# The first two-level projection loads its fourth weight part into batch 1's turned x, ahead of its first product

## The chip, the cores and the metric

The kernel runs on one core of one Trainium2 chip. The metric is device time in microseconds (us) for one execution of the whole kernel. In what follows TensorE does the matrix products, VectorE and ScalarE the elementwise work and the copies out of the product banks, and SyncE and ScalarE each issue DMAs on a queue of their own. GpSimd has little to do here.

## The reference

An attention without softmax is followed by a feed-forward net of products. All of it is in 32-bit floats; the weights come in as 64-bit floats and are converted in the kernel.

```
# q, k, v: (8 batches, 8 heads, 576 tokens, 64)
kv  = einsum('bhsd,bhse->bhde', k, v)
out = einsum('bhsd,bhde->bhse', q, kv)
x   = out / sqrt(mean(out*out, axis=-1) + 1e-6) * g_norm     # -> x: (4608 tokens, 512)
a   = x @ w1                                                 # w1, w2: (512, 1024)
b   = x @ w2
h   = a * b @ w3                                             # w3: (1024, 1024)
result = h @ w_out                                           # w_out: (1024, 512)
```

## The kernel before

**The algebra.** The kernel folds w3 and w_out into one 1024 x 512 matrix (`w3o_sb`) at the start, so per token only two steps are left: the gates (x times w1 and w2, and the product of the two) and the projection (times the folded matrix). Both use Strassen's scheme in Winograd's form: seven block products in place of eight, with sums of blocks made on VectorE. From batch 2 on parts of the gates, and from batch 1 on the whole projection, apply the scheme on two levels: each of the seven outer products is itself made of seven inner ones.

**The groups.** The tokens are worked off in nine groups of 512: the first 512 tokens of each of the eight batches, and one group made of the 64 last tokens of every batch. The loop over `groups` runs the gates of group T, then its projection, and in the gaps of both (`between`, and slots hung on single copies) the attention of the next batch: k·v, q·kv, the norm, and the turning of x and q into the layout in which TensorE wants them. The turning goes through DMA transposes: `turn_by_dma` splits the words into planes by a copy (L321 or L323), SyncE issues the transpose (L325), and a copy puts the words together again (L335).

**The first two-level projection.** Group 0 (batch 0) is projected on one level. While that runs, `prepare_b` makes from the folded matrix the seven right-hand sides of the outer products, each with the sums that its inner products need, and stores them to HBM (`w3o_l2`), seven parts of 128 x 1792 words, 896 KB. Every later projection reads these parts back, one for each outer product, in order. The first projection to do so is batch 1's (T = 1), `project_twice` with `done[T] = 0`. Counting the products from 1, product i reads part i.

**The homes of the parts.** `streams` holds three homes of part size: two in the old place of `w3o_sb` (streams 0 and 1) and one in a `raw` tile (stream 2). A home is free for the next part when the product that read it is done. From the second projection on there is a fourth home: the turned x of the batch whose gates have just ended (`xT[...]`), which takes the fourth part at the start of the projection. Batch 1's xT is read by the matmuls of the gates (L778), for the last time in the product of a12 and b21, the last but one of the stage. Its buffer goes to batch 3's x later.

**Who issues a part.** `load_b` issues the next part each time it is called (L1248). In the first projection parts 4 and 6 go out on ScalarE's queue and the others on SyncE's; the first three are issued well ahead, within the gates of T = 1.

**The order.** SyncE, TensorE and GpSimd run their instructions in the order in which the kernel writes them. VectorE does so too in the last part of the gates and in the projection. ScalarE's instructions are put in order by a scheduler, when the kernel is built. Each engine takes its own in that order, so what stands behind a waiting instruction waits too. DMAs share eight completion semaphores in turn; a DMA also waits for the one that held its semaphore before.

**Around the projection.** The lines that the steps touch are these. `copy_seven` (L1121, L1122) copies the two product banks of an outer product to `slots`; a product that writes these banks again waits for it. `gates` ends with c21: ScalarE copies one half (L946), VectorE multiplies (L948). VectorE then makes the left-hand sums of the inner products (L1284 to L1287, and L858, L859), and, between them, the sums of the next batch's x (L848). After a product VectorE adds its banks to the sums kept before (L1125, L1126). After the fourth product SyncE issues loads of q for the batch after next (L95), and after the fifth to the seventh it loads weight parts of the next group's gates (L1018).

The kernel's order of one projection, without what is the same:

```
        if done[T]:
            load_b()
        r1 = products(0)
        ...
        products(3, r2)
        if not done[T]:
            load_b()
```

Of the kernel before, what the change touches and what calls it, by code (L numbers as in the profile page):

```python
# [22 lines left out]
def kernel(  # L23
# [711 lines left out]
    def w3_by_dma(c):  # L735
        natural, to = chunks[:, c, 0, :], place_w3(1, c).rearrange("p m f -> p (m f)")
        return turn_by_dma(
            [natural], to, natural, [to], nc.scalar.copy, split=nc.vector.tensor_copy
        )
# [131 lines left out]
    o_sbs, ab_sums, w3o_sums, streams, inner_sums, in_a_row = [], [], [], [], [], []  # L871
# [172 lines left out]
    def gates_of_two(T, between=lambda: None):  # L1044
# [36 lines left out]
        def load(w, n):  # L1081
            last = max(at for (v, m, _), at in BLOCKS.items() if (v, m) <= (w, n))
            if last + 1 >= (len(loaded_w) - len(streams) + 1) * IN_PART:
                load_w()
            if (w, n) == (1, len(PRODUCTS) - 1):
                for _ in range(3):
                    load_b()
# [146 lines left out]
    def load_b():  # L1234
        n = len(loaded_b)
        if n == ALL_B:
            return
        i = n % 7
        t = streams[n % 3] if n < 7 else streams[(i + 1 if i < 3 else i) % 3]
        if n >= 7 and i == 3:  # L1240
            done_with = xT[groups[1 + n // 7]]
            t = done_with.rearrange("p i j r n -> p (i j r n)")[:, 0:PART]

        part = {ALL_B - 2: 6, ALL_B - 1: 7}.get(n, n % 7)

        queue = nc.scalar if i in ((3, 5) if n < 7 else (4, 6)) else nc.sync
        if n + 1 < ALL_B:
            queue.dma_start(out=t, in_=w3o_l2[part])  # L1248
        else:
            t = t[:, 0:1024]  # L1250
            queue.dma_start(out=t, in_=w3o_l2[part, :, 0:1024])
        loaded_b.append(t)
# [43 lines left out]
    def project_twice(T, last, ahead, load_after):  # L1296
# [12 lines left out]
        def products(n, ps=None):  # L1309

            new = ps is None or n == 5 or last and n == 6
            if ps is None:
                ps = [bank(ps_mm, "mm").rearrange("p (i n) -> p i n", n=P) for _ in range(2)]
            a11, a12, a22, s1, s2, s4, s3 = inner[n]
            w = loaded_b[7 * done[T] + (5 if last and n == 6 else n)]
            b = w[:, 0:1024].rearrange("p (f n) -> p f n", n=N)
            b11, t3, b21, b22 = (
                b[:, 2 * i:2 * i + 2, j * P:(j + 1) * P] for i in range(2) for j in range(2)
            )
            t1, t2, t4 = (  # L1320
                w[:, 1024 + 256 * i:1280 + 256 * i].rearrange("p (c n) -> p c n", n=P)
                for i in range(3)
            )
            seen = set()
            for place, x, y in (
                (0, a11, b11), (3, a12, b21), (1, a22, t4), (2, s1, t1), (6, s2, t2), (5, s4, b22),
                (4, s3, t3),
            ):
                for c in range(2):
                    nc.tensor.matmul(  # L1330
                        ps[place // 4][:, place % 4, :], lhsT=x[:, c, :], rhs=y[:, c, :],
                        start=new and place // 4 not in seen,
                        stop=(c == 1),
                        skip_group_check=True,
                    )
                    seen.add(place // 4)
            return ps
# [41 lines left out]
                store_block(0, 0, m, m + 1, queue, cols)  # L1379


        if done[T]:
            load_b()
        r1 = products(0)
        p1 = keep("p1", r1)
        load_b()
        r2 = products(1)
        p5 = keep("p5", r2)
# [6 lines left out]
        for f in ahead:  # L1395
            f()
        products(3, r2)
        if not done[T]:
            load_b()
        for f, *args in slots.pop(("proj", "loads"), []):  # L1400
            f(*args)
        if last:
# [29 lines left out]
    done = {}  # L1432
# [14 lines left out]
    with tc.manual_schedule(  # L1447
# [63 lines left out]
        for c in range(KF):  # L1511
# [9 lines left out]
            if c < KF - 2:  # L1521
# [12 lines left out]
                if c in SPLIT:  # L1534
                    t = turns[SPLIT[c]] = w3_by_dma(SPLIT[c])
# [49 lines left out]
    for n, T in enumerate(groups):  # L1585
# [119 lines left out]
        if T:  # L1705
            project_twice(
                T, last, [] if last else combine_x(groups[n + 1]),
                load_w if not last and groups[n + 1] in IN_TWO else load_b,
            )
            in_order.__exit__(None, None, None)  # L1710
            continue
# [46 lines left out]
```

## Time and profile before

| | |
|---|---|
| median of 3 runs | 739.49 us (738.42 to 739.94) |
| profiled execution | 738.91 us, of which the span is 736.8 us |
| TensorE busy in the span | 731.3 us, 99% |
| VectorE, ScalarE, GpSimd busy | 85%, 52%, 3% |
| granted TensorE clock | 1.000 |
| DMA | 170.44 MB, mean 231 GB/s |
| weight parts from `w3o_l2` (L1248), 896 KB each | 40 on SyncE, 15 on ScalarE; 4.4 to 8.7 us from issue to landing |

The profile is one execution, taken by the hardware profiler. Rows of the timeline give the start in us from the start of the span, the length, the engine, the line and the tiles (written <- read); "SPq" and "ACTq" are DMA issues on SyncE's and ScalarE's queue, where the length is that of the issue and not of the transfer. In brackets stands how long the engine was idle before, and what ended that. The ends of matmuls are modelled.

### The profile page before, as it was taken

Reading aid. Unit: us, or ns where it says so; the run is one execution under the profiler, and the core shown is the slowest. Engines: PE = TensorE matmul, PEld = TensorE weight load, DVE = VectorE, ACT = ScalarE, POOL = GpSimd, SP = SyncE. Lnnn points to the kernel's source line nnn. Section 1 sums busy time; section 2 is a strip of 40 time slices with the busy share of each in tenths; the row PEclk is TensorE's granted clock in tenths of the full one; section 3 lists DMA queues with packets and bytes.
Section 4 is the critical chain, followed back from the end, with each engine's and each line's share of the span. In section 5 each row is a group of like instructions: output and inputs, shape, how many; then the busy total and the mean of one; then the engine's idle time right before and its main releaser. Section 6 shows DMA issues by size and latency. Waiting matters only on the chain.

```text
span 736.8 us, 16930 instructions
## 1 busy us (share of the span) xinstructions
PE 731.3 (99%) x6873; PEld 658.4 (89%) x6873; DVE 627.5 (85%) x1259; ACT 381.1 (52%) x660; POOL 23.1 (3%) x30
## 2 busy tenths in 40 slices
PE   8999999999999999999999999999999999999998
PEld 6455788888899999999999999999999999999998
DVE  7988898868879689969996899689879987997797
ACT  7888778315652676167517761675177313212321
POOL 0000000220001000000010001000001000000000
PEclk9999999999999999999999999999999999999999
DMA  8999925599999598869987988698748862565454
GB/s 309 355 338 249 285 94 154 157 329 274 326 299 321 172 286 245 277 159 276 259 275 166 302 237 278 157 299 242 253 115 217 221 209 87 187 214 158 135 196 142
DMA packets 138769, 170.44 MB, mean 231 GB/s; under 512 B 81220, under 2 KB 114116, under 8 KB 138692
## 3 DMA queue, kind: packets, MB, share of 16 engines
q1 hardware_dynamic: 136240, 155.02, 71.4%
q10 hardware_dynamic: 2452, 14.35, 5.8%
q8 instruction: 54, 0.88, 0.5%
q14 instruction: 23, 0.19, 0.1%
HBM read 130.55 MB, written 20.71 MB: 205 GB/s over the span
## 4 chain that ended last, share of the span: by engine, by line
PE 98%; DMA 1%; DVE 0%; SPq 0%; issue 0%; ACT 0%; DVEq 0%
PE mm L778 37%; PE mm L1330 23%; PE mm L1072 21%; PE mm L747 8%; PE at L778 3%; PE at L362 3%; PE mm L440 1%; PE at L440 1%; PE at L731 1%; DMA raw<-in_moe_w_out_dram 1%; PE at L1373 0%; PE at L459 0%; PE at L382 0%; PE mm L302 0%; SPq L219 0%; PE at L476 0%
## 5 line engine op out<-in xcount | busy, mean ns | idle before, releaser
L1121 ACT COPY slots<-mm 128x512 f32<-128x512 f32 x88 | 51.6, 586 | 127.3 <-PE mm L1330 83.1
L778 PE MATMUL mm<-xT,w_sb 128*128 128x256 f32 x432 | 99.3, 379 | 0.0
L778 PEld LDWEIGHTS mm<-xT,w_sb 128*128 128x128 f32 x432 | 81.4, 190 | 11.1 <-issue 0.5
L778 PE MATMUL mm<-xc,ws 128*128 128x256 f32 x328 | 74.4, 379 | 0.0
L778 PEld LDWEIGHTS mm<-xc,ws 128*128 128x128 f32 x328 | 62.3, 190 | 8.5
L796 ACT COPY slots<-mm 128x512 f32<-128x512 f32 x58 | 34.0, 585 | 69.5 <-PE mm L778 64.7
L747 PE MATMUL mm<-chunks,ab 128*128 128x512 f32 (+1 forms) x136 | 59.2, 573 | 0.3 <-DVE chunks L193 0.3
L1125 DVE TENSOR_TENSOR slots<-mm,slots 128x512 f32<-128x512 f32 x66 | 45.2, 685 | 16.3 <-PE mm L1072 15.9
L1122 ACT COPY slots<-mm 128x384 f32<-128x384 f32 x88 | 42.3, 481 | 25.0 <-PE mm L1330 22.1
L1072 PE MATMUL mm<-ws,w3o_sb 128*128 128x128 f32 x350 | 54.0, 275 | 0.0
L1330 PE MATMUL mm<-w3o_sb,ab 128*128 128x128 f32 x368 | 48.8, 276 | 0.0
L408 DVE TENSOR_REDUCE inv<-sq 128x8 f32<-128x512 f32 (+1 forms) x40 | 24.6, 629 | 26.9 <-ACT sq L407 26.9
L1072 PEld LDWEIGHTS mm<-ws,w3o_sb 128*128 128x128 f32 x350 | 46.4, 192 | 0.0
L1330 PEld LDWEIGHTS mm<-w3o_sb,ab 128*128 128x128 f32 x368 | 45.4, 192 | 0.5
L1330 PE MATMUL mm<-w3o_sb,raw 128*128 128x128 f32 x340 | 43.5, 275 | 0.0
L747 PEld LDWEIGHTS mm<-chunks,ab 128*128 128x128 f32 x136 | 24.0, 190 | 21.0 <-issue 17.9
L1330 PEld LDWEIGHTS mm<-w3o_sb,raw 128*128 128x128 f32 x340 | 40.7, 192 | 0.0
L778 PE MATMUL mm<-xT,ws 128*128 128x256 f32 x160 | 38.1, 381 | 0.0
L1126 DVE TENSOR_TENSOR slots<-mm,slots 128x384 f32<-128x384 f32 x66 | 36.3, 551 | 2.0 <-PE mm L1330 1.9
L778 PE MATMUL mm<-xc,w_sb 128*128 128x256 f32 x152 | 36.6, 384 | 0.0
L778 PEld LDWEIGHTS mm<-xT,ws 128*128 128x128 f32 x160 | 30.1, 190 | 4.3 <-ACT slots L796 0.2
L335 ACT COPY xT<-xn 128x1024 uint16<-128x1024 uint16 x26 | 30.2, 1167 | 3.5 <-DMA xn<-xT 3.5
(247 smaller groups left out, 1664.3 us busy)
## 6 DMA issues: line engine op xcount, KB each, us to landing
w3o_sb<-w_l SPq DMA_DIRECT2D x21, 896.0 KB, 6.2
w3o_sb<-w3o_l SPq DMA_DIRECT2D x18, 896.0 KB, 6.6
raw<-in_moe_w_dram SPq DMA_DIRECT2D x31, 512.0 KB, 7.8
raw<-w3o_l SPq DMA_DIRECT2D x15, 896.0 KB, 4.9
w3o_sb<-w3o_l ACTq DMA_DIRECT2D x14, 896.0 KB, 4.8
k_sb<-in_k_dram SPq DMA_DIRECT2D x16, 576.0 KB, 4.9
v_sb<-in_v_dram SPq DMA_DIRECT2D x16, 576.0 KB, 5.8
q_sb<-in_q_dram SPq DMA_DIRECT2D x32, 256.0 KB, 5.4
```

The source lines that it names most:

```text
L335: copy(words(dst), src)
L362: nc.tensor.matmul(ps[r * D:(r + 1) * D, :], lhsT=k_sb[rows, r, cols], rhs=v_sb[rows, r, cols], start=(j == 0), stop=(j == JS - 1),)
L408: adds["norm"] = nc.vector.tensor_reduce(out=inv[:, i], in_=sq.rearrange("p (h d) -> p h d", d=D), axis=AX.X, op=ALU.add)
L747: nc.tensor.matmul(sums_ps[half][m][:, cols], lhsT=w3T[half, c][:, m, :], rhs=chunks[:, c, 1, cols], start=(c == 0 and cols.start == 0), s ...
L778: nc.tensor.matmul(ps[:, u, :], lhsT=lhsT(a_name, u, c), rhs=rhs(b_name, c),  start=(u == 0 and c == 0 and new), stop=(c == chunks - 1), s ...
L796: copies.setdefault(name, []).append(nc.scalar.copy(t, ps))
L1072: nc.tensor.matmul(ps[place // 4][:, place % 4, :], lhsT=x, rhs=y, start=new and place // 4 not in seen, stop=True, skip_group_check=True,)
L1121: nc.scalar.copy(z[:, 0:4], ps[0])
L1122: return nc.scalar.copy(z[:, 4:7], ps[1][:, 0:3])
L1125: nc.vector.tensor_add(z[:, 0:4], ps[0], z[:, 0:4])
L1126: nc.vector.tensor_add(z[:, 4:7], ps[1][:, 0:3], z[:, 4:7])
L1330: nc.tensor.matmul(ps[place // 4][:, place % 4, :], lhsT=x[:, c, :], rhs=y[:, c, :], start=new and place // 4 not in seen, stop=(c == 1), ...
```

## The change

In the first two-level projection the fourth part is loaded into the home of batch 1's turned x, and the load is issued ahead of the first product in place of after it. The first three parts change homes (streams 1, 2, 0 in place of 0, 1, 2), so that each later part finds its home free one product sooner: part 5 after product 1, part 6 after product 2, part 7 after product 3. The call after the fourth product goes. Queues (ScalarE for parts 4 and 6) and the order of the parts stay. The later projections are as before.

```diff
     def load_b():
         n = len(loaded_b)
         if n == ALL_B:
             return
         i = n % 7
-        t = streams[n % 3] if n < 7 else streams[(i + 1 if i < 3 else i) % 3]
-        if n >= 7 and i == 3:
+        t = streams[(i + 1 if i < 3 else i) % 3]
+        if i == 3:
             done_with = xT[groups[1 + n // 7]]
             t = done_with.rearrange("p i j r n -> p (i j r n)")[:, 0:PART]
...
-        if done[T]:
-            load_b()
+        load_b()
         r1 = products(0)
         p1 = keep("p1", r1)
         load_b()
...
         products(3, r2)
-        if not done[T]:
-            load_b()
         for f, *args in slots.pop(("proj", "loads"), []):
             f(*args)
```

In the built program this moves two instructions on ScalarE and none on SyncE. Part 4's issue stands on ScalarE ahead of the L946 copy of c21, where it stood behind the second L335 copy of x; part 6's issue stands ahead of the copies after product 3, where it stood behind the two L335 copies of q that follow them. On SyncE parts 5 and 7 keep their places and wait for one product less.

## The prediction

> **What bounds the kernel now.** I read the page first, for the bound. Its chain of waits says TensorE:
>
> ```profile
> PE 98%; DMA 1%; DVE 0%; SPq 0%; issue 0%; ACT 0%; DVEq 0%
> ```
>
> Then the same chain in order of time, cut to the edited stage. Columns: start, length, what:
>
> ```profile
> 204.83 6.04 PE mm L778 x28
> 210.87 21.89 PE mm L1330 x196
> 232.75 3.46 PE mm L778 x16
> ```
>
> Nothing stands between these pieces. The first projection (196 matmul records, seven products of 28) runs from 210.87 to 232.75 in 21.89 us; the undisturbed ones at 283.49 and 643.64 take 21.93 and 21.88. So no part of the weights comes late in this execution, and an earlier load has no TensorE idle time to remove. The price, if any, must come from queues that the moved loads share. So I read ScalarE and SyncE in this window (start, length, engine, line, tiles; "q" is the issue of a DMA):
>
> ```profile
> 210.95 0.37 ACT L946 COPY c<-mm 128x256 f32<-128x256 f32 x1 [4.42 <-PE mm L778]
> 213.54 1.16 ACT L335 COPY xT<-xn 128x1024 uint16<-128x1024 uint16 x1 [2.22 <-DMA xn<-xT]
> 214.09 0.36 ACTq L1248 DMA_DIRECT2D w3o_sb<-w3o_l  x1
> 214.60 0.58 ACT L1121 COPY slots<-mm 128x512 f32<-128x512 f32 x1
> ```
>
> ```profile
> 198.30 5.36 SPq L325 DMA_TRANSPOSE xn_left<-qT_left  x1
> ...
> 207.01 4.31 SPq L325 DMA_TRANSPOSE xn<-xT  x2
> 211.42 2.61 SPq L325 DMA_TRANSPOSE q_sb<-qT  x2
> 217.15 6.58 SPq L1248 DMA_DIRECT2D w3o_sb<-w3o_l  x2
> ```
>
> ScalarE's 213.54 row is the one to see: it waits 2.22 us for two transposing DMAs, and behind it in its order stand the copies (L1121, L1122) that empty product 1's banks. Last, VectorE, which has little air:
>
> ```profile
> 212.30 0.41 DVE L948 TENSOR_TENSOR ab<-c,mm 128x256 f32<-128x256 f32 x1
> 212.63 0.68 DVE L1284 TENSOR_TENSOR inner_sums<-raw 128x512 f32<-128x512 f32 x1
> ...
> 214.68 0.68 DVE L1287 TENSOR_TENSOR raw<-raw 128x512 f32<-128x512 f32 x1
> ```
>
> **What the old timing leaves.** I count products from 1; each lasts 3.13 us, and by TensorE's rows they start at 210.71, 213.83, 216.96, 220.08, 223.21, 226.34 and 229.46. Issue plus landing (DMA issues of that stretch): part 4, 214.09 + 5.0 = 219.1; part 5, 217.15 + 4.6 = 221.8; part 6, 220.45 + 4.9 = 225.4; part 7, issued at 217.15 + 6.58 - 0.34 = 223.39, + 5.4 = 228.8. The margins are 1.0, 1.4, 0.9 and 0.7 us: thin, all positive.
>
> **The edits.** *First three parts.* The same three loads of 896 KB stand at the same place of SyncE's order (196.16 to 197.86), in other homes. Cost 0.
>
> *Part 4's load.* It moves to ScalarE's order ahead of the L946 copy. The changed program's order gives its waits: the last product that reads batch 1's xT (the last but one of that stage, ended by 210.87 - 1.73 = 209.14), and the landing of the xn_left transpose, with which it shares a completion semaphore. That one is issued at 198.30 and takes 12.0 us (DMA issues), so 210.3. The issue then goes at 210.3 instead of 214.09. No row shows ScalarE issuing a DMA while SyncE is inside a transpose. Near bound: the 0.36 of row 214.09, done at 210.7, before the L946 copy can start (210.95): 0. Far bound: it stands until SyncE's transposes are issued (211.42 + 2.61 = 214.03), and the copy is 3.1 us late. Who waits for that: VectorE's product at L948 has 212.30 - (210.95 + 0.37) = 0.98 us to spare, and the four sums behind it end at 214.68 + 0.68 = 215.36 for a block that TensorE starts at 216.51, 1.15 more. So 2.1 of the 3.1 us are free and 1.0 would stop product 2. I take 0, since the nearest row is an issue of this very size on this very queue.
>
> *Its data.* The old load's 896 KB came after the transposes: the DMA rate is 279 GB/s at 212 to 213, falls to 112 at 215 to 216, and is 421 at 216.5 to 218. Issue to data is about 1.0 us, so the data now starts near 211.4, on top of the second xn transpose and the two of q. Those move 128x1024 two-byte words each, 262 KB, about 1.0 us at 257 to 287 GB/s. Bounds for their delay: 0, if the load gets only what the transposes leave; above, if it goes wholly first, 3.0 us, its time from data start to 218.1 in the old place; at its full rate of 421 GB/s, 917 KB / 421 = 2.2. The L335 copy would start that much after 213.54. From there to the end of the first bank's copy (214.60 + 0.58 = 215.18) nothing can shrink, and product 3, which writes that bank again, starts at 216.96. So 1.78 us of delay are free, and the rest stops TensorE one for one: 0 to 1.2 us. I take 2.1, just under the full-rate value: 2.1 - 1.78 = 0.3 us. Next in line are the subtractions that read xT (VectorE, 219.39, L848; the second L335 copy ends at 216.63: 2.8 spare) and q's copies (220.66, behind a product-3 copy): both hidden.
>
> The Trainium skill speaks against mixing these two. "DMA: Bandwidth & Descriptors", section "Queues, rings and completion order", says that each DMA engine goes round-robin, packet by packet, over the queues with work; so a load from ScalarE's queue would take its turn beside SyncE's transposes and not wait behind them. Read as equal shares, the 1.65 us of transposes left at 211.4 would take 3.3, a delay of 1.65 and no stall: the sum would be 0.0 instead of 0.3. No row of this trace has both queues full at once.
>
> *Part 6's issue* (ScalarE) now stands ahead of product 3's first copy, L1121 at 219.00, before which ScalarE idles 1.36 us; 0.36 fits in. Without that cover it would cost 0.36. *Parts 5 and 7* (SyncE) pass no other instruction, they only wait for a product one earlier. Behind part 7 stand the two q loads (223.84), which may go about 1 us sooner. *The home:* batch 3's x is written there only in the next stage, after 232.75; part 4 is read out at 223.2. All three cost 0.
>
> **Sum.** The profiled execution took 738.91 us, 736.82 of span (736.8 on the page) and 2.09 around it. 738.91 + 0.3 = 739.2. The median of the runs shown is 0.58 above it: 739.49 + 0.3 = **739.8**. A measurement of this kernel tells about 0.2% from no change, 1.48 us, so the borders are 738.0 and 741.0.
>
> **The rivals.** *Transposes stand behind the load (slower).* One mechanism: the xn transposes are held on the DMA queues. Up to 1.78 us it is free; it decides from 1.78 + 1.48 = 3.3 us. The bound above gives 3.0 if only the data is held. If the issue of the second transpose is stretched as well, as the pair of 207.01 was (4.31 us against 2.59 at 277.20, 1.7 more), it is 4.7: 2.9 of stall, 742.4 as the worst, 741.6 in the middle. For it: DMA busy 1.13 from 211 to 215. Against: the second transpose is already issued at 211.33. Chance 0.18.
>
> *ScalarE held by the issue.* 3.1 us late, 1.0 lost: 740.5. Against: both old issues took 0.36; for: none of them was beside a transpose. Chance 0.14, within the border.
>
> *Late parts elsewhere (faster).* In other executions a part may come after its product, at margins of 0.7 to 1.4; the change adds some 3 us to each. The spread of the runs is 738.42 to 739.94, so this is worth at most 739.49 - 738.42 = 1.07: 738.4, still inside the border. Past it the chance is 0.06, since the profiled execution, itself near the fast end, shows no stall that could go. I give the case 0.12 in all.
>
> *It does not do what it says.* Were part 4 held until 214.03, it would go when it went before; parts 5 to 7 are earlier all the same. Time 739.5 plus the ScalarE price just counted; it is the same case as that rival.
>
> **Numbers.** Forecast (0 to 0.6 us more, no measurable change) 0.56; transposes 0.18; ScalarE held 0.14; late parts 0.12. Faster by over 0.2%: 0.06. Slower: 0.18, the first rival. Within: 0.56 + 0.14 + 0.06 = 0.76. The range must leave out no more than 0.2: from 738.6, near the faster case, to 741.3, which takes in the ScalarE rival and the near half of the transposes' one.
>
> **What would show it.** In the profile of the changed kernel: a DMA issue of L1248 on ScalarE near 210.3, under 0.5 us long, with the L946 copy still at about 210.95. The L335 copy's wait for the transposes grows from 2.22 us to between 3.9 and 4.3. Seven products in 21.9 to 22.5 us, any gap ahead of the third, none ahead of the fourth to seventh. I am wrong if the projection is over 23.4 us long (the slower rival), if a gap stands ahead of the second product (ScalarE held), or if the time falls under 738.0 with no TensorE gap gone.

## The result, and the profile after

The changed kernel takes 740.61 us (median of 15 runs, 739.24 to 743.81), the kernel before 739.09 us in the same comparison (15 runs, 738.42 to 740.57). The ratio is 1.0024, 95% interval 1.0015 to 1.0034: about 1.5 us slower, a little past the 0.2% that the prediction took as its border. The profiled execution of the changed kernel took 743.56 us (span 741.5), so it is one of its two slowest; the sizes below are checked on four more profiles.

Page of the changed kernel, the chain of waits by engine, and the group of TensorE that now waits:

```profile
PE 97%; DMA 2%; DVE 0%; ACT 0%; issue 0%; SPq 0%; ACTq 0%; DVEq 0%
...
L1330 PE MATMUL mm<-w3o_sb,raw 128*128 128x128 f32 x320 | 42.0, 279 | 3.0 <-ACT slots L1121 3.0
```

The chain in order of time around the first projection:

```profile
204.88 5.84 PE mm L778 x27
...
210.94 7.91 DMA q_sb<-qT
218.85 0.49 issue
219.34 0.59 ACT slots L1121
219.93 0.04 issue
219.97 17.52 PE mm L1330 x140
```

Of the seven products five (140 records) now stand behind a wait. The third starts at 219.97 instead of 216.96. The chain names the transposes of q, which landed last before the copy; that is an inference from times, and the moved copies below show that it is the x transposes. ScalarE's timeline has the real order:

```profile
209.96 0.38 ACTq L1248 DMA_DIRECT2D xT<-w3o_l  x1
210.79 0.37 ACT L946 COPY c<-mm 128x256 f32<-128x256 f32 x1 [4.42 <-PE mm L778]
218.27 1.16 ACT L335 COPY xT<-xn 128x1024 uint16<-128x1024 uint16 x1 [7.11 <-DMA xn<-xT]
...
219.34 0.58 ACT L1121 COPY slots<-mm 128x512 f32<-128x512 f32 x1
```

Part 4 is issued at 209.96, in 0.38 us; the L946 copy is as punctual as before. But the wait for the x transposes grew from 2.22 to 7.11 us, and product 1's copy (L1121) stands behind it. It is the second of the two x transposes that is held: the first lands 5.4 us after its issue in both kernels, the second after 8.6 us instead of 3.4. SyncE, same kernel:

```profile
206.61 4.23 SPq L325 DMA_TRANSPOSE xn<-xT  x2
210.94 6.89 SPq L325 DMA_TRANSPOSE q_sb<-qT  x2
```

Even the issue of q's transposes stretches, from 2.61 to 6.89 us. What happens on the DMA engines shows in the queues' packets between 213 and 215 us (q10 is ScalarE's queue, q1 SyncE's; packets, MB, share of the 16 engines):

```profile
q10 hardware_dynamic: 67, 0.48, 86.6%
q1 hardware_dynamic: 69, 0.02, 13.5%
```

Read from these counts, the queues take turns, one packet each: 67 of the load's packets and 69 of the transposes'. But a packet of the load has 7,168 bytes (0.48 MB / 67) and one of the transposes 256. Before the change, with the transposes alone, 1,123 packets of SyncE's queue passed in one microsecond (212 to 213); and when the load was alone there (217 to 218), 60 of its packets did:

```profile
q1 hardware_dynamic: 1123, 0.28, 124.1%
...
q10 hardware_dynamic: 60, 0.43, 103.6%
```

As long as the load lasts the transposes all but stand still. The load suffers as well: 7.6 us from issue to landing instead of 5.0. The transposes' turns do not account for that, since they fill only 13.5% of the engines. Each packet of the load itself takes longer: 86.6% of 16 engines in 2 us, over 67 packets, is 0.41 us for one, where the load alone has 0.28. No run says why.

Last, TensorE in the windows of the gap and of product 3; behind each engine's busy time its count, then PEclk, DMA share and GB/s:

```profile
216.90:220.00 3.10, 0.09 (x2) 0.03 (x1) 2.81 (x7) 1.73 (x3) 0.00 (x0) 1.00 1.21 209
220.00:224.80 4.80, 4.80 (x28) 4.80 (x29) 1.89 (x3) 2.81 (x5) 0.00 (x0) 0.64 0.88 362
```

After the gap the granted clock is 0.64 and product 3 takes 224.83 - 219.97 = 4.86 us instead of 3.13. Gap 3.01 and clock 1.73 make 4.74 of the 4.7 us by which the span grew (741.5 against 736.8). TensorE waits for another engine nowhere else between 80 and 736 us.

### The profile page after: what moved, and what is told of

Its sections match the earlier page's. It is cut to its first block, busy times and chain, and to the rows that moved or that the text cites. A ratio compares the mean times of both kernels' runs of the same rounds, so it can differ in the third digit from the quotient of the medians.

```text
span 741.5 us, 16932 instructions
## 1 busy us (share of the span) xinstructions
PE 733.3 (99%) x6873; PEld 660.3 (89%) x6873; DVE 627.5 (85%) x1259; ACT 381.3 (51%) x660; POOL 23.0 (3%) x30
## 4 chain that ended last, share of the span: by engine, by line
PE 97%; DMA 2%; DVE 0%; ACT 0%; issue 0%; SPq 0%; ACTq 0%; DVEq 0%
PE mm L778 37%; PE mm L1330 23%; PE mm L1072 21%; PE mm L747 8%; PE at L778 3%; PE at L362 3%; PE mm L440 1%; DMA q_sb<-qT 1%; PE at L440 1%; PE at L731 1%; DMA raw<-in_moe_w_dram 1%; PE at L1373 0%; PE at L459 0%; PE mm L302 0%; PE at L382 0%
## 5 line engine op out<-in xcount | busy, mean ns | idle before, releaser
L1121 ACT COPY slots<-mm 128x512 f32<-128x512 f32 x88 | 51.7, 587 | 126.6 <-PE mm L1330 82.9
L408 DVE TENSOR_REDUCE inv<-sq 128x8 f32<-128x512 f32 (+1 forms) x40 | 24.6, 629 | 27.1 <-ACT sq L407 27.1
L1330 PE MATMUL mm<-w3o_sb,raw 128*128 128x128 f32 x320 | 42.0, 279 | 3.0 <-ACT slots L1121 3.0
L1330 PEld LDWEIGHTS mm<-w3o_sb,raw 128*128 128x128 f32 x320 | 39.1, 195 | 3.2 <-ACT slots L1121 3.2
L335 ACT COPY xT<-xn 128x1024 uint16<-128x1024 uint16 x26 | 30.3, 1168 | 8.4 <-DMA xn<-xT 8.4
```

Source lines behind the costliest of these rows:

```text
L335: copy(words(dst), src)
L408: adds["norm"] = nc.vector.tensor_reduce(out=inv[:, i], in_=sq.rearrange("p (h d) -> p h d", d=D), axis=AX.X, op=ALU.add)
L1121: nc.scalar.copy(z[:, 0:4], ps[0])
L1330: nc.tensor.matmul(ps[place // 4][:, place % 4, :], lhsT=x[:, c, :], rhs=y[:, c, :], start=new and place // 4 not in seen, stop=(c == 1), ...
```

## The experiments

**The changed kernel again, four more profiles.** No edit.

> The changed kernel once more, for a second profile. Theory (transposes held): ScalarE's load and SyncE's transposes take turns on the DMA engines, so the L335 copy starts 3 to 5 us later than the 213.54 of before, and the third product starts late by that delay less 1.8 us; the gap differs from execution to execution, and where it is over some 2 us the matmuls after it are slower for a while. Rival (a gap of another origin, such as a late weight part): the gap stands ahead of another product, or the L335 copy is on time. Time 739.2 to 743.8 us.

> A third profile of the changed kernel. Theory: delay of the L335 copy less 1.78 us is the gap ahead of product 3 (first two profiles: 4.9 and 3.6 us, gaps 3.0 and 1.95); matmuls slower after a gap of 1.9 us or more. Time 739.2 to 743.8 us.

> The changed kernel again, for a profile of an execution at full granted clock, as 13 of its 15 timed ones were (739.2 to 741.6 us; the two at 0.998 took 743.6 and 743.8). Theory (the loss is the gap ahead of product 3, and a lower clock after it only in some executions): at clock 1.000 a gap of 0.5 to 2 us and product 3 at 3.1 us. Rival (the loss at full clock is elsewhere): no gap, or a smaller one than the loss.

> As the run before it: a second chance of an execution at full granted clock; same expectations.

The time from the start of the L946 copy to the start of the first L335 copy (2.59 us in the profile of before) says how late the transposes are; the prediction's 1.78 us should be free:

| profile | L946 to L335 | over before, less 1.78 | gap before product 3 | clock | span | time |
|---|---|---|---|---|---|---|
| the first | 7.48 | 3.11 | 3.01 | 0.998 | 741.5 | 743.56 |
| again | 6.41 | 2.04 | 1.95 | 0.998 | 740.1 | 742.12 |
| again_2 | 7.10 | 2.73 | 2.62 | 0.998 | 741.8 | 743.94 |
| again_3 | 6.79 | 2.42 | 2.31 | 1.000 | 738.9 | 740.92 |
| again_4 | 7.25 | 2.88 | 2.78 | 0.998 | 741.2 | 743.26 |

The gap follows the delay to 0.1 us five times out of five. The third repetition is the one at full clock, where the loss is the gap alone:

```profile
219.07 1.60 PE L1330 MATMUL mm<-w3o_sb,raw 128*128 128x128 f32 x12 [2.31 <-ACT slots L1121]
220.51 1.50 PE L1330 MATMUL mm<-w3o_sb,inner_sums 128*128 128x128 f32 x12
```

The 15 timed runs part in the same way: 13 have a granted clock of 1.000 and take 739.24 to 741.64 us, two have 0.998 and take 743.56 and 743.81. My expectation that a gap from some 2 us on slows the matmuls was too simple: 1.95 did, 2.31 did not.

**Part 4 on SyncE's queue.**

```diff
-        queue = nc.scalar if i in ((3, 5) if n < 7 else (4, 6)) else nc.sync
+        queue = nc.scalar if i in ((5,) if n < 7 else (4, 6)) else nc.sync
```

> The changed kernel with part 4 issued on SyncE in place of ScalarE, so behind all four transposes; homes and the earlier parts 5 to 7 stay. Theory (transposes held by a load on the other queue): no gap ahead of the third product, L335 copy at 213.5 as before, time within 0.1% of before, ratio 0.999 to 1.001. Rival (the new homes, or the earlier parts 5 to 7, cost the time): stays at 1.002 against before.

738.50 us (11 runs) against 738.76 for the kernel before, ratio 0.9999 (0.9990 to 1.0007). Part 4 is issued at 212.95, behind the four transposes. Counted from the start of the first product that is 2.75 us, still sooner than the 3.38 of before the change. It lands 5.1 us later. The L335 copy is on time, and the projection is whole again:

```profile
212.36 1.17 ACT L335 COPY xT<-xn 128x1024 uint16<-128x1024 uint16 x1 [1.55 <-DMA xn<-xT]
```

```profile
210.36 21.88 PE mm L1330 x196
```

The new homes and the earlier parts 5 to 7 are all in this kernel; they cost nothing, and bring nothing that can be measured.

**Part 4 on ScalarE, but as late as before.** The call before the first product goes for this projection; part 4 is issued behind product 1's copies and the second L335 copy.

```diff
-        load_b()
+        if done[T]:
+            load_b()
+        else:
+            slots.setdefault(("proj", "p1"), []).append((load_b,))
         r1 = products(0)
```

> The changed kernel with part 4 still on ScalarE's queue and still in batch 1's turned x, but issued behind the second L335 copy, where it was before (near 214.1); parts 5 to 7 stay one product earlier. Theory: no gap, ratio to before 0.999 to 1.001. Rival (the home in xT costs, or the earlier parts 5 to 7): 1.002.

739.80 us (11 runs), ratio 1.0013 (1.0004 to 1.0022): half of the expectation failed. There is no gap ahead of product 3, and the L335 copy starts 1.61 us after the L946 copy; but there is one ahead of product 4:

```profile
221.19 1.58 PE L1330 MATMUL mm<-xT,raw 128*128 128x128 f32 x12 [1.39 <-DMA xT<-w3o_l]
```

Part 4 went out on ScalarE at 213.60 and part 5, now one product earlier, on SyncE at 213.58. The packets from 216 to 219 us:

```profile
q1 hardware_dynamic: 83, 0.59, 47.9%
q10 hardware_dynamic: 83, 0.59, 47.0%
```

Turns again, this time between equal packets, so each load gets half. A packet takes 0.27 us here (47.0% of 16 engines in 3 us, over 83), as in a load alone: it is beside the transposes that the packets grew slower. They land after 7.3 and 7.5 us, part 4 too late for product 4. So an earlier part 5 is not free in itself: on SyncE's queue alone part 4 goes first, on two queues the part that is needed first shares with the one that is not.

**The load alone.** The kernel before, with one more load of part 4 on ScalarE ahead of the L946 copy, into batch 1's turned x, where nobody reads it.

```diff
         if done[T]:
             load_b()
+        else:
+            home = xT[groups[1]].rearrange("p i j r n -> p (i j r n)")[:, 0:PART]
+            nc.scalar.dma_start(out=home, in_=w3o_l2[3])
         r1 = products(0)
```

> The kernel before, unchanged in its parts and homes, with one more load of 896 KB on ScalarE's queue ahead of the L946 copy, into batch 1's turned x, which nobody reads. Theory: this load alone makes the loss; the L335 copy 3 to 5 us late, a gap ahead of the third product, ratio to before 1.001 to 1.004, as the change has. Rival (homes or parts 5 to 7): ratio 0.999 to 1.001.

742.98 us (6 runs, 740.16 to 745.94), ratio 1.0057 (1.0035 to 1.0079): more than the change itself. The trace has two gaps, ahead of products 3 and 4:

```profile
219.28 1.60 PE L1330 MATMUL mm<-raw 128*128 128x128 f32 x12 [1.52 <-ACT slots L1121]
...
225.21 1.58 PE L1330 MATMUL mm<-w3o_sb,raw 128*128 128x128 f32 x12 [2.53 <-DMA w3o_sb<-w3o_l]
```

The first is the change's: L946 to L335 takes 5.99 us, 3.40 over before, less 1.78 is 1.62, and the gap is 1.52. With homes and parts as before, the early load on the other queue suffices. The second is its consequence: the true part 4 stands on ScalarE behind the late L335 copy (issued at 217.73 instead of 214.09) and goes out together with part 5, as in the experiment above.

**The same load at a quarter and at half of its bytes.** `PART // 4` and `PART // 2` columns, to columns of the same home from 1024 on.

> The kernel before with an extra load on ScalarE's queue ahead of the L946 copy, as in the full extra load, but of a quarter of its bytes (128 packets of 1792 B). By turns packet by packet, 8 on each DMA engine: they hold the transposes by the wait for the first (about 1.1 us) and 8 x 0.07 us, 1.7 in all, so within the 1.78 us that are free: ratio 0.999 to 1.001, L335 copy at 214.5 to 215.5. Rival (any load there holds the transposes for some 4 us whatever its size): 1.002 and a gap ahead of product 3.

> The same with half of the bytes (packets of 3584 B, 0.14 us each): 1.1 + 1.1 = 2.2 to 2.6 us of delay, a gap of 0.4 to 0.8 us ahead of product 3, ratio 1.000 to 1.002. Rival (whatever its size): a gap as with the full extra load, 1.5 us or more.

738.76 us (12 runs), ratio 1.0001 (0.9993 to 1.0010), and 738.62 us (10 runs), ratio 0.9999 (0.9989 to 1.0008). L946 to L335 is 2.92 and 3.45 us; neither kernel has a gap. So size does count, but I had both delays too large (the half should have left a gap of 0.4 to 0.8). Against the two kernels that have nothing beside the x transposes (1.92 with part 4 on SyncE, 1.61 with part 4 later) they are some 1.2 and 1.7 us; against the profile of before, 0.3 and 0.9. The full load adds 4.1 to 4.4 against those two, and 3.4 against the profile of before. By either measure it adds more than twice what the half adds, and I have no run that says why. The two measures differ by 0.7 to 1.0 us, so the delays of the small loads are known no better than that.

**The x copies moved out of the way.** The changed kernel with both L335 copies of batch 2's second half of x behind the copies after product 2.

```diff
-            (1, (("p3", "p1"), ("p3", "p5")), (("p3", "c21"), ("proj", "p1"))),
+            (1, (("p3", "p1"), ("p3", "p5")), (
+                (("proj", "p5"), ("proj", "p5")) if b == FIRST_OF_TWO
+                else (("p3", "c21"), ("proj", "p1"))
+            )),
```

> The changed kernel, part 4 early on ScalarE as there, with the two L335 copies of batch 2's x moved behind the copies after product 2 (and so behind product 1's copies). Theory (the loss goes through ScalarE's order: late transposes, L335 copy, product 1's copies, product 3): the transposes land as late as in the change, the L335 copies start at 216.5 to 218.3, but no gap ahead of product 3; the x sums on VectorE up to 1.5 us late, hidden; ratio to before 0.999 to 1.001. Rival (late transposes cost by another way, or the load slows something else): 1.002.

738.71 us (12 runs) against 738.65, ratio 1.0003 (0.9994 to 1.0012). The x transposes take 6.1 us to land (4.4 before the change, 7.0 in it), and q's issue still takes 5.80; yet TensorE runs through, since product 1's copies no longer stand behind them:

```profile
212.87 0.59 ACT L1124 COPY slots<-mm 128x512 f32<-128x512 f32 x1 [1.37 <-PE mm L1333]
...
217.71 1.16 ACT L335 COPY xT<-xn 128x1024 uint16<-128x1024 uint16 x1
...
211.05 21.88 PE mm L1333 x196
```

(The lines of this kernel are three higher; the last row is from its chain.) The late transposes cost only through ScalarE's order. No kernel tried is measurably faster than the one before.

## Why the prediction was right or wrong

*The range and the bound.* 740.61 lies within 738.6 to 741.3, in part by luck. Four of the five profiled executions took 742.1 to 743.9, above the range and three of them above the 742.4 that the rival had as its worst; the median lies inside because nine of the 15 timed runs took less than the fastest profile. The prediction's own sign of the slower rival, a projection over 23.4 us long, came in every profile: 24.6 to 27.0 us by TensorE's rows, against 22.0 before. That TensorE had nothing to gain held: the two versions that keep the earlier loads and lose the collision come out at 0.9999 and 1.0003.

*The likeliest case was not the one that came.* I forecast 0.3 us more, with 0.56 on it, and 0.18 on the first rival, transposes held behind the load. The mechanism, the place (a gap ahead of the third product and no other) and the 1.78 us that are free were right. What failed is one term, "Its data": the delay. I took 2.1 with an upper bound of 3.0 us; the five profiles have 3.8 to 4.9 over before. The step was to let the load go first at its own pace and to count its 3.0 us. In the trace it takes turns with the transposes packet by packet, which all but gives it the engines, and its own packets take 0.41 us instead of 0.28; so it lasts 7.6 us to its landing instead of 5.0 while they hardly move. The bound of two transfers that share must count both as slowed, and mine slowed only one; why the load's packets grow slower stays open. The rival's upper delay, 4.7 us, is near the measured ones by chance: it came from a stretched issue of the second x transpose, and the issue of the x pair took 3.65 to 4.23 us in the five profiles, no longer than the 4.31 of before. The prediction put the L335 copy's wait at 3.9 to 4.3 us; it was 6.0 to 7.1.

*The rule that I weighed, I read wrongly.* The Trainium skill ("DMA: Bandwidth & Descriptors", section "Queues, rings and completion order") says that an engine goes round-robin over the queues, a packet at a time. The 67 and 69 packets, and the 83 and 83, agree. I made equal shares of the time out of it, and a sum of 0.0 (from 1.65 us of transposes left, which I took from no row); turns are equal, not times, and against 7,168 bytes a turn of 256 is little. The page speaks of packets of several descriptors; here the profile's records come out one for one.

*Missing from the sum:* the granted clock. After the gap four of five profiles ran product 3 at about half clock for a while, 1.6 to 1.7 us more; two of the 15 timed runs did. The prediction had no such term.

*Confirmed:* part 4's issue at 209.96 (forecast 210.3) in 0.38 us, so the rival of ScalarE held by the issue is out; part 6's issue and the home cost nothing (part 4 on SyncE has both). That parts 5 and 7 cost nothing held in the change, but not as a rule: beside a part 4 on the other queue an earlier part 5 cost 1.39 us. The rival of late parts elsewhere, a gain, did not show.

*Open:* the five profiles lost 2.1 to 5.0 us of span and the timed runs 1.5 in the median. The timed runs at full clock reach down to 739.24, so there the collision must be smaller; no profile caught such an execution. Why four of the five profiled executions show the lower clock, and two of the 15 timed ones, is open too.

## What to carry to other kernels

In these runs a load on another queue did not go behind a running transfer but in turns with it (67 packets to 69), and where its packets were large (7,168 bytes) and the other's small (256), the small ones waited. So ask what is in flight on every queue at the new time, not only whether the queue at hand is free. Then follow the delayed transfer to the engine that waits for it, and look at what stands behind it in that engine's order: here the copy that was late had nothing to do with the loads. When TensorE shows no gap, an earlier load has none to remove, and can still cost time; if one is wanted for margin, put it on the queue that carries the transfers it must not disturb, behind them (here 0.9999 instead of 1.0024).

## What the runs showed of the hardware

- Two queues with work passed equal numbers of packets through the DMA engines: 67 to 69 between 7,168 and 256 bytes, 83 to 83 between equal ones. A packet of 7,168 bytes took 0.41 us beside the transposes, 0.27 beside an equal load and 0.28 alone.
- Gaps of TensorE of 1.95, 2.62, 2.78 and 3.01 us were followed by a granted clock near half (0.50 to 0.57 over some 3 us); gaps of 1.39, 1.52, 2.31 and 2.53 were not, so the length of the gap alone does not decide it. In the fourth repetition the clock is 0.50 from 219.85 to 222.85 and 0.93 after. The Trainium skill ("TensorE: Matmul & The Clock Gate", section "Why this matters for your kernels") warns of idle gaps over about 3 us; here shorter ones sufficed. Its section "Part 1: The HAM clock gate" has a free-running window of 3.4 us and half rate when idle. Half rate for such a window would cost 1.7 us, as an estimate from that page; the measured costs are 1.6 to 1.7.
- DMA transposes on SyncE took 6.89 us to issue instead of 2.61 while a load on ScalarE's queue was in flight; ScalarE's own issue took 0.38 us.
